# Linear attention followed by a feed-forward layer: GpSimd's tangent products moved into their own chunk, a new order of chunks 3 to 6, and batch 1's attention bursts one group later

## The chip, the cores and the metric

The kernel runs on one core of a Trainium2 chip. The metric is the time of one execution in microseconds, as the device measures it; the kernel before takes 278.01 us (median of three runs, 277.81 to 278.37). Its profiled execution took 277.38 us, of which 275.6 lie between the first and the last instruction. Positions such as "39.01" are microseconds from the first instruction.

## The reference

Eight batches, eight heads, 576 positions, head size 64. The attention is linear: ReLU on q and k, each multiplied by the cosine and by the sine of its position, then two matrix products in place of a softmax. The result is the input of a feed-forward layer with a Swish that has a factor per column.

```
theta = pi/2 * pos / S
phi(x) = concat(relu(x)*cos(theta), relu(x)*sin(theta))
kv  = phi(k)^T v ;  z = sum over positions of phi(k)
x   = (phi(q) kv) / (phi(q) z + 1e-6)          # 4608 tokens x 512
h   = x @ w_in                                  # 512 -> 2048
g   = h * sigmoid(beta * h)
out = g @ w_out                                 # 2048 -> 512
```

## The kernel before

The 4608 tokens go through the layer in 9 chunks of 512. Beside chunk c the attention of a later batch is done: its pieces are put between the groups of the layer, so that TensorE always has something to do. Names used below:

- A *group* (or slot) of the layer's first half is one tile of 128 hidden columns: four matmuls of 512 columns, then Silu on ScalarE. In chunk 0, slots 0 to 15 are these, and slots 16 to 31 are the output matmuls. From slot 24 on, slot s uses row block s - 16 of `w_out`, four matmuls of 512 columns.
- The *kv burst* (`kv_mm`) is 72 small matmuls that form phi(k)^T v of a batch; `kv_take` copies the result out of PSUM.
- The *transposes of q* (`q_turn_pe`) put q into the layout that the next step needs; the *takes* copy them out, ScalarE as they are (`qts`) and VectorE multiplied by the tangent (`qs`). In later batches the DMA transposes (`q_turn_dma`), and the tangent product is an instruction of its own (`q_tan`, two for a batch, on GpSimd).
- The *num burst* (`num_mm`, `num_all`) multiplies q by kv. The division (`x_rden`, `x_mul`, or `x_part`) follows on VectorE, and a transpose gives `xt`, the input of the layer.
- `cast_out(j)` turns block j of `w_out` from f32 to bf16, scaled by 1/beta, on VectorE, or with "a" on ScalarE.

From chunk 1 on, the products of the layer use a scheme with seven products of half size in place of eight (`o_fast`, `h_fast`), for which sums of blocks are formed on VectorE: `g_sum` (of g), `x_sum` (of x), `wh_sums` (of w_in).

The instructions of one engine keep the order in which the kernel lists them. This is batch 1's attention in chunk 0 (cuts marked):

```python
def rest():                      # called in slot 4
    ...
    load_w("out", 0); load_w("out", 1)
    load_raw(1, "v"); load_raw(1, "k"); load_raw(1, "q")
    load_w("out", 2, 2)          # blocks 8 to 11, in two loads
    load_w("out", 3, 2)
    ...
    for j in range(8):
        cast_out(j)
    v_scale(1, 0); k_relu(1)
    q_relu(1, 0); q_relu(1, 1)   # VectorE

def second():
    takes.append(q_turn_pe(1, 0, 4, hold=True))
    takes.append(q_turn_pe(1, 1, 6, hold=True))
    cast_out(8)
    takes[0]("act", 0)
    takes[0]("dve", 1)
    cast_out(9, "a")
    takes[0]("dve", 0)
    takes[0]("act", 1)
    cast_out(10)
    for e, i in (("act", 0), ("dve", 1), ("act", 1), ("dve", 0)):
        takes[1](e, i)
    for j in (11, 12, 14, 15):
        cast_out(j, "a")

for slot in range(32):
    ...
    else:                                        # slots 24 to 31
        for tt in range(4):
            o_mm(0, tt, (slot - 16,))            # reads wout block slot - 16
    ...
    if slot in early:
        early[slot]()                            # after the slot's matmuls
```

Chunk 2 begins with plain groups and ends with the two output halves x and y. Its end reads (cuts marked):

```python
y["5"](); y["c5"]()
if c == FAST - 1:
    x_sums(c + 1)
    wh_sums(12)
...
y["2"](); y["a2"]()
y["7"](); y["a7"]()              # VectorE adds out of PSUM
v_half(b + 1, 0, 5, 7)
y["3"](); y["a3"]()
v_half(b + 1, 0, 7, 9)
v_half(b + 1, 1, 3, 9, "act")
y["4"](); y["c4"]()              # the product 4 adds to the bank that a7 has read
```

Chunks 3 to 6 are given by one string of operations, `ORDER`. In it `p0` to `p7` are plain groups and `sp0` to `sp7` their Silus; `X1` to `X7` (and Y, Z, V) are the seven products of a quick pair of groups, with their copies and adds (`c1X`, `c5X`, `cuX`, `a2X`, `a3X`, `a7X`) and Silus (`SaX`, `SbX`); `K`, `kt` are the kv burst and its copy; `s01` to `s34` are the sums of g, `t1` to `t4` those of x for the next chunk; `N0` is the num burst, `x0` to `x2` the divisions; `ox1` and so on are products of the output; `k`, `q`, `v`, `w` prepare later batches; `g0`, `g1` are GpSimd's tangent products. These are held back until a named instruction is done:

```python
def q_tan(b, jp, behind=None):
    got = tan_mul(nc.gpsimd, qs_of(b)[:, jp], qts[b % 2][:, jp], 0, NQ)
    if behind is not None:
        tc.add_manual_dep(got.ins, behind.ins.name, ..., reason="GpSimd behind the sums")
```

Of the kernel before, what the change touches and what calls it, by code (L numbers as in the profile page):

```python
# [17 lines left out]
NQ = 9  # L18
# [4 lines left out]
def kernel(  # L23
# [16 lines left out]
    B, H, S, D = q.shape  # L40
# [76 lines left out]
    def cast_out(j, eng="d"):  # L117
        i, jj = divmod(j, 4)
        st = stages["out", i]
        if eng == "a":  # L120
            nc.scalar.activation(wout[:, j, :], st[:, jj, :], AF.Copy, scale=rbeta[:, j : j + 1])
        else:
            nc.vector.tensor_scalar(wout[:, j, :], st[:, jj, :],
                                    scalar1=rbeta[:, j : j + 1], scalar2=None, op0=ALU.mult)
# [141 lines left out]
    def kv_mm(b, jp, bank, jjs=(0, 1)):  # L266
        t = kv_out(jp, bank)
        for n in range(NQ):
            for jj in jjs:
                for g in range(2):  # L270
                    hs = slice(g * HP, (g + 1) * HP)
                    nc.tensor.matmul(  # L272
                        t[jj * HP : (jj + 1) * HP, g], lhsT=rk[hs, n, 2 * jp + jj, :],
                        rhs=vb[hs, n, 2 * jp + jj].rearrange("q s e -> q (s e)"),
                        start=(n == 0), stop=(n == NQ - 1))
# [382 lines left out]
    got = x_rden(2, 0, 0, 7, (0,))  # L658
# [55 lines left out]
    def num_seven(jp, bank):  # L714
        for n in range(7):
            num_mm(1, n, jp, bank, n)
# [3 lines left out]
    def second():  # L720

        takes.append(q_turn_pe(1, 0, 4, hold=True))
        takes.append(q_turn_pe(1, 1, 6, hold=True))
        cast_out(8)
        takes[0]("act", 0)
        takes[0]("dve", 1)
        cast_out(9, "a")
# [7 lines that stand above are left out]
# [1 line left out]
    early = {  # L736
        4: lambda: (num_mm(0, 8, 0, 2, 0), num_mm(0, 8, 1, 2, 1), rest()),
        15: lambda: v_scale(1, 1, eng="act"),
        22: lambda: (kv_mm(1, 0, 6), kv_mm(1, 1, 6), kv_take((0, 1), 6, "act")),
        23: second,  # L740
        25: lambda: (num_seven(0, 4), x_mul(x_rden(4, 0, 0, 7, (0,)), 0, 7), cast_out(13)),
        26: lambda: (num_seven(1, 6), x_mul(x_rden(6, 0, 0, 7, (1,)), 0, 7)),
        28: lambda: x_turn_pe(1, 0, 7, 4, ("act",), (0,)),
        29: lambda: x_turn_pe(1, 0, 7, 5, ("dve",), (1,)),
    }

    def num_rest():
# [23 lines left out]
        if b + 1 < B:  # L771
            load_raw(b + 1, "k")

    def kv_all(b, bank=6):
        kv_mm(b, 0, bank)
        kv_mm(b, 1, bank)
        kv_take((0, 1), bank)

    def x_part(b, t, bank):
        x_div(t, bank)  # L780
# [30 lines left out]
    for slot in range(16):  # L811
        h_group(1, slot)
        if slot == 0:
            num_rest()
            att_q(2)
            v_half(2, 0)
        if 3 <= slot < NQ:
            v_half(2, 1, slot, slot + 1, "act")
        if slot == 4:
            k_all(2)  # L820
            v_half(2, 1, 0, 3)
        elif slot == 6:
            w_sums()
        elif slot == 11:
            kv_all(2)
            for jp in range(2):
                tan_mul(nc.vector, qs_of(2)[:, jp], qts[0][:, jp], 0, NQ)
    q_relu(3, 0, "act")
# [28 lines left out]
    got = wh_sums(0)  # L857
# [9 lines left out]
    def k_piece(b, j):  # L867
# [4 lines left out]
            load_raw(b + 1, "k")  # L872

    ORDER = (
        "p0 Y1 X1 c1X p1 X5 c5X sp0 X6 X2 K c1Y X3 cuX kt Y6 X7 p2 a2X a3X Y5 sp1 a7X cuY c5Y Y7 Z1 SaX "
        "X4 c1Z p3 Y3 Y2 SbX sp2 a7Y Z2 s01 Y4 Z5 sp3 Z6 s03 a3Y a2Z p4 SbY V1 a2Y c5Z cuZ Z7 s02 a7Z p5 "
        "SaY c1V V6 Z3 s11 sp4 s12 cuV a3Z V2 Z4 s14 sp5 V5 SbZ c5V V7 p6 a2V V3 SaZ a7V a3V s21 sp6 SaV "
        "p7 s04 s13 V4 s22 SbV s23 sp7 s24 s31 s33 N0 k1 s32 ox1 c1o ox5 k3 c5o k2 ox6 s34 g0 g1 x0 k0 "
        "ox3 oy1 cuo c1y x2 o3x ox2 ox7 v8 oy5 x1 c5y o2x oy6 w8 q0 q1 cuy v2 v6 oy3 o7x v3 w1 oy7 w4 w3 "
        "w7 o7y ox4 v5 t3 w5 oy2 v4 c4x o3y v7 t1 w0 oy4 w6 t2 v1 c4y v0 o2y w2 t4")  # L880
    ORDER_LAST = (
        "E1 c1E E2 F1 X1 a2E c1X c1F X5 X2 E5 X6 c5X E6 cuX c5E cuE X3 a2X Y1 E3 X7 a3X c1Y a3E SaX a7X "
        "E7 SaE F6 Y5 F5 a7E X4 Y2 c5F Y6 SbX F2 F3 a2Y c5Y a2F cuF E4 Z1 Y3 cuY SbE c1Z a3F Y7 F7 a3Y "
# [40 lines left out]
    def chunk(c, b, x, y, parts):  # L924
        steady = {"X": (0, 2, 0, 1), "Y": (4, 3, 4, 5), "Z": (8, 0, 2, 1), "V": (12, 4, 3, 5)}
        end = {"X": (0, 6, 0, 1), "E": (2, 5, 3, 4), "Y": (4, 2, 0, 1), "F": (6, 7, 3, 4), "Z": (8, 6, 0, 1),
               "V": (12, 5, 3, 4)}
        pairs = {n: h_fast(c, at[0], at[1:]) for n, at in (steady if b < B else end).items()}

        def plain_bank(n):  # L930
            return (2 if n == 7 else 6 + n % 2) if b < B else (2, 7)[n % 2]

        plain = [2, 3, 6, 7, 10, 11, 14, 15]
        outs = {"x": x, "y": y}

        def q_next():
            if b + 3 < B:
                load_raw(b + 3, "q")

        def raw_next(name):  # L940
            if b + 2 < B:
                load_raw(b + 2, name)

        xs_all = {"x0", "x1", "x2"}
        take = prep(b, [
            ({"k0", "k1", "k2", "k3"} | xs_all, lambda: raw_next("k")),
            ({"q0", "q1"} | xs_all, q_next),
            ({f"{o}{n}" for o in "vw" for n in range(NQ)}, lambda: raw_next("v"))])
        last_sum = None
        for op in (ORDER if b < B else ORDER_END if c + 1 < NTC else ORDER_LAST).split():  # L950
            n = int(op[-1]) if op[-1].isdigit() else None
            if op == "K":
                kv_mm(b, 0, 4)
                kv_mm(b, 1, 4)
            elif op == "kt":
                kv_take((0, 1), 4)
            elif op[0] == "N":
                for t, bank in enumerate(parts):
                    num_all(b, t, bank)
            elif op[0] == "x":  # L960
                x_part(b, n, parts[n])
                take(op)
            elif op[0] in "kvwq":
                take(op)
            elif op[0] == "t":
                if c + 1 < NTC:
                    x_sum(c + 1, n)
            elif op[0] == "g":
                if b + 1 < B:
                    q_tan(b + 1, n, None if n else last_sum)  # L970
            elif op[0] == "p":
                h_plain(c, plain[n], plain_bank(n), 2 if n < SPLITS.get(c, (0, 0))[0] else 1)
            elif op[:2] == "sp":
                h_silu(c, plain[n], plain_bank(n))
            elif op[0] == "o" and n is not None:
                outs[op[1]][op[2]]()
            elif op[0] == "o":
                outs[op[2]]["a" + op[1]]()
            elif op[0] == "c" and op[2] in "xyo":
                outs["x" if op[2] == "o" else op[2]][op[:2]]()  # L980
            elif op[0] == "s":
                last_sum = g_sum(c, 2 * int(op[1]), 2 * int(op[1]) + 2, n)
            else:
                pair = op[0] if op[0] in pairs else op[-1]
                pairs[pair][op.replace(pair, "")]()
        if b + 2 < B:
            q_turn_dma(b + 2)

    def h_first(c):
        b = c + 1  # L990
        for slot in range(16):
            h_group(c, slot, 2 if slot < SPLITS.get(c, (0, 0))[0] else 1)
            if c == 2:
                if slot == 0:
                    k_all(b)
                    v_half(b, 1, 0, 4)
                if 1 <= slot < 6:
                    v_half(b, 1, slot + 3, slot + 4, "act")
                if slot == 3:
                    att_q(b + 1)  # L1000
                    wh_sums(4)
                if slot == 9:
                    wh_sums(8)
            if slot == (8 if c == 2 else 1):
                kv_all(b)
            if slot in (3, 7, 11):
                g_sums(c, slot // 2 - 1, slot // 2 + 1)
            elif slot in (13, 15):
                sums = g_sums(c, slot // 2, slot // 2 + 1)
        return sums  # L1010

    FAST = 3
    for c in range(2, NTC):
# [4 lines left out]
        if c >= FAST:  # L1018
            chunk(c, b, x, y, parts)
            continue  # L1020
        sums = h_first(c)
        for t, bank in enumerate(parts):
            num_all(b, t, bank)
        q_tan(b + 1, 0, sums)
        q_tan(b + 1, 1)
        for i, n in enumerate("156273"):
            x[n]()
            if n in "156":
# [15 lines left out]
        y["c5"]()  # L1044
        if c == FAST - 1:
            x_sums(c + 1)
            wh_sums(12)
        v_half(b + 1, 1, 2, 3, "act")
        y["6"]()
        y["cu"]()  # L1050
# [5 lines left out]
        y["3"]()  # L1056
        y["a3"]()
        v_half(b + 1, 0, 7, 9)
        v_half(b + 1, 1, 3, 9, "act")
        y["4"]()  # L1060
        y["c4"]()
# [31 lines left out]
```

## Time and profile before

| what | value |
|---|---|
| time, median of three | 278.01 us |
| span of the profiled execution | 275.6 us |
| busy: TensorE, VectorE, ScalarE, GpSimd | 268.9, 221.0, 184.6, 67.8 us |
| mean granted clock of TensorE | 1.000 |
| one tangent product of a batch half | 2.38 us on GpSimd, 1.35 on VectorE |

How to read the profile lines that follow. A timeline line has the start, the time from the start to the end of the last of the merged instructions, the engine, the line of the kernel, the operation, what it writes and reads, the shapes, and the number of instructions. In brackets stand the idle time of the engine ahead of it and the instruction that ended that idle time. Matmuls are pipelined, so one matmul's stated duration is longer than the distance to the next; the distance is what counts. `PE` is TensorE, `DVE` VectorE, `ACT` ScalarE, `POOL` GpSimd, and `SP` issues DMAs.

### The profile page before, as it was taken

The numbers are of one execution on the slowest core, as the hardware profiler recorded it, in microseconds if no ns is written. First come the engines' busy times: TensorE is split into PE (matmuls) and PEld (weight loads), VectorE is DVE, ScalarE is ACT, GpSimd is POOL, SyncE is SP. The second block draws the span as 40 slices with busy tenths as digits, with TensorE's granted clock in tenths as the row PEclk, the third lists the DMA queues.
The fourth block names the chain that finished last, engine by engine and source line by source line (L and its number), as shares of the span: only waits on it lengthen the run. The fifth ranks groups of instructions, "written<-read, shape, count | busy, mean of one in ns | idle before, by whom it ended". The sixth has DMA issues, their size and how long they took to land.

```text
span 275.6 us, 9047 instructions
## 1 busy us (share of the span) xinstructions
PE 268.9 (98%) x3749; PEld 199.8 (73%) x3749; DVE 221.0 (80%) x578; ACT 184.6 (67%) x381; POOL 67.8 (25%) x87
## 2 busy tenths in 40 slices
PE   8899999999999999999999999999999999999993
PEld 8554455446875599869866998688768886888683
DVE  5989968599999898599959995899589589558851
ACT  5778757797248657697669756976694289429821
POOL 1444000600087073106420552044300140000000
PEclk9999999999999999999999999999999999999999
DMA  7999999999969999961899199915400640033005
GB/s 248 369 394 382 393 389 312 375 193 377 244 153 309 245 309 295 394 130 38 179 359 267 39 220 301 121 21 107 114 2 12 117 115 2 0 70 86 2 24 130
DMA packets 50745, 54.00 MB, mean 196 GB/s; under 512 B 31232, under 2 KB 31760, under 8 KB 50704
## 3 DMA queue, kind: packets, MB, share of 16 engines
q1 hardware_dynamic: 47744, 45.88, 59.5%
q0 software_dynamic: 2688, 7.34, 8.9%
q8 instruction: 29, 0.48, 0.7%
q10 hardware_dynamic: 272, 0.21, 0.3%
q14 instruction: 12, 0.10, 0.2%
HBM read 36.71 MB, written 9.44 MB: 167 GB/s over the span
## 4 chain that ended last, share of the span: by engine, by line
PE 83%; DMA 12%; DVE 2%; ACT 1%; SPq 1%; issue 0%; ACTq 0%; DVEq 0%
PE ps L547 35%; PE ps L468 16%; PE ps L422 13%; PE ps L380 10%; DMA raw_q<-in_q_dram 7%; DMA w_stage<-in_moe_w_in_dram 5%; PE ps L293 4%; PE ps L517 3%; PE ps L272 2%; DVE win L115 1%; ACT vb L217 1%; SPq L79 1%; PE ps L234 0%; PE ps L352 0%; DVE qb L194 0%
## 5 line engine op out<-in xcount | busy, mean ns | idle before, releaser
L413 ACT ACTIVATE g_t<-ps,beta 128x512 bf16<-128x512 f32 x96 | 61.0, 698 | 3.1 <-DVE ps L498 2.8
L547 PEld LDWEIGHTS <-S 128*128 128x128 bf16 x589 | 51.3, 98 | 5.0
L510 POOL DMA_DIRECT2D out_dram<-o_sb x56 | 33.5, 604 | 66.3 <-ACT o_sb L523 24.6
L380 PE MATMUL ps<-xt,win 128*128 128x512 bf16 (+1 forms) x196 | 42.8, 375 | 0.1
L547 PEld LDWEIGHTS <-g_t 128*128 128x128 bf16 x440 | 38.2, 98 | 4.3 <-issue 0.3
L422 PE MATMUL ps<-xt,win 128*128 128x512 bf16 (+1 forms) x184 | 40.8, 351 | 0.0
L388 ACT ACTIVATE g_t<-ps,beta 128x512 bf16<-128x512 f32 x48 | 32.2, 690 | 8.0 <-PE ps L380 7.8
L380 PEld LDWEIGHTS <-win 128*128 128x128 bf16 x196 | 18.8, 98 | 21.0 <-issue 0.4
L547 PE MATMUL ps<-wout,g_t 128*128 128x256 bf16 (+1 forms) x284 | 31.7, 262 | 0.0
L547 PE MATMUL ps<-wout,S 128*128 128x256 bf16 (+1 forms) x305 | 31.5, 255 | 0.0
L547 PE MATMUL ps<-T,S 128*128 128x256 bf16 (+1 forms) x284 | 30.8, 262 | 0.0
L399 DVE TENSOR_TENSOR S<-g_t 128x512 bf16<-128x512 bf16 (+1 forms) x66 | 25.1, 409 | 3.6 <-ACT g_t L413 2.7
L217 ACT ACTIVATE vb<-raw_v,sin 128x256 bf16<-128x256 f32 (+1 forms) x61 | 27.4, 501 | 0.9 <-DMA raw_v<-in_v_dram 0.9
L222 POOL TENSOR_TENSOR qs<-qt,tanr 128x1152 bf16<-128x1152 bf16 x6 | 14.2, 2382 | 50.8 <-DVE den L304 29.8
L468 PEld LDWEIGHTS <-w_stage 128*128 128x128 bf16 x224 | 21.6, 98 | 6.7
L468 PE MATMUL ps<-w_stage 128*128 128x256 bf16 x168 | 26.2, 272 | 0.0
L422 PEld LDWEIGHTS <-win 128*128 128x128 bf16 x184 | 17.9, 98 | 10.1
L315 DVE TENSOR_TENSOR xs<-ps,rden 128x768 bf16<-128x768 f32 (+4 forms) x26 | 22.8, 883 | 0.8
L219 DVE TENSOR_SCALAR vb<-raw_v,cos 128x256 bf16<-128x256 f32 x63 | 20.5, 380 | 0.1
L468 PEld LDWEIGHTS <-win 128*128 128x128 bf16 x168 | 16.4, 98 | 4.8 <-issue 0.3
L468 PE MATMUL ps<-xt,win 128*128 128x256 bf16 x112 | 19.1, 273 | 0.0
L594 ACT COPY p<-ps 128x256 f32<-128x256 f32 x16 | 6.0, 373 | 17.0 <-PE ps L547 16.9
(105 smaller groups left out, 417.6 us busy)
## 6 DMA issues: line engine op xcount, KB each, us to landing
raw_v<-in_v_dram SPq DMA_DIRECT2D x7, 1152.0 KB, 9.9
raw_k<-in_k_dram SPq DMA_DIRECT2D x7, 1152.0 KB, 7.5
raw_q<-in_q_dram SPq DMA_DIRECT2D x7, 1152.0 KB, 7.7
out_dram<-o_sb POOLq DMA_DIRECT2D x56, 128.0 KB, 4.4
w_stage<-in_moe_w_in_dram SPq DMA_DIRECT2D x3, 1024.0 KB, 13.0
w_stage<-in_moe_w_out_dram SPq DMA_DIRECT2D x2, 1024.0 KB, 8.1
w_stage<-in_moe_w_out_dram SPq DMA_DIRECT2D x4, 512.0 KB, 11.9
out_dram<-o_sb SPq DMA_DIRECT2D x12, 128.0 KB, 2.4
```

The costliest lines, as they stand in the source:

```text
L217: nc.scalar.activation(o, a, AF.Copy, scale=t[:, n : n + 1])
L219: nc.vector.tensor_scalar(o, a, scalar1=t[:, n : n + 1], scalar2=None, op0=ALU.mult)
L222: return eng.tensor_tensor(dst.rearrange("q n (g p) -> q n g p", g=2), src.rearrange("q n (g p) -> q n g p", g=2), tanr[:, n0:n1].unsqueez ...
L315: nc.vector.tensor_tensor(o.rearrange("q j n s d -> q j (n s) d"), nv[:, :, a:z, :, 0:D].rearrange("q j n s d -> q j (n s) d"), rden[:, :, ...
L380: nc.tensor.matmul(ps[:, h_bank(c, jt), i * 64 : (i + w) * 64], lhsT=win[jt // 4][:, mi, (jt % 4) * P : (jt % 4 + 1) * P], rhs=xt[:, i : i ...
L388: nc.scalar.activation(gs[c, jt // 4][:, jt % 4], ps[:, h_bank(c, jt)], AF.Silu, scale=beta[:, jt : jt + 1])
L399: return nc.vector.tensor_tensor(o, l, r, op=op)
L413: nc.scalar.activation(gs[c, jt // 4][:, jt % 4], ps[:, bank], AF.Silu, scale=beta[:, jt : jt + 1])
L422: nc.tensor.matmul(ps[:, bank, o * 64 : z * 64], lhsT=win[jt // 4][:, mi, (jt % 4) * P : (jt % 4 + 1) * P], rhs=xt[:, o:z, jp, g * HP : (g ...
L468: nc.tensor.matmul(dst, lhsT=left[:, g], rhs=right[:, :, g * HP : (g + 1) * HP], start=start and g == 0, stop=stop and g == 1, skip_group_ ...
L510: (eng or own).dma_start(out=out_v[bb, n][:, m0:m1], in_=o_sb[hf * HP : (hf + 1) * HP, m0:m1])
L547: nc.tensor.matmul(dst[:, m : m + w], lhsT=left(i), rhs=right[:, i, m : m + w], start=start and i == 0, stop=stop and i == order[-1], skip ...
```

## The change

GpSimd's two tangent products of a batch were made in the output stage of the chunk before, behind the last sum of g. Now they are made in the batch's own chunk, near its beginning, behind the copy `c5X`, at a time when VectorE works out of PSUM. The string for chunks 3 to 6 is a new one with the same operations. In chunk 0, the kv burst of batch 1, its q transposes, num bursts and x transposes each move one slot later, so that a late arrival of q does not hold them up; `cast_out(8)`, which slot 24 needs, moves ahead of slot 24. In chunk 1 the kv burst of batch 2 moves one slot earlier and its copy from VectorE to ScalarE, and two scalings of v from ScalarE to VectorE. At the end of chunk 2 `wh_sums(12)` moves behind the adds.

The diff, cut to its core:

```diff
@@ second()
         takes.append(q_turn_pe(1, 0, 4, hold=True))
         takes.append(q_turn_pe(1, 1, 6, hold=True))
-        cast_out(8)
         takes[0]("act", 0)
@@ early
-        22: lambda: (kv_mm(1, 0, 6), kv_mm(1, 1, 6), kv_take((0, 1), 6, "act")),
-        23: second,
-        25: lambda: (num_seven(0, 4), x_mul(x_rden(4, 0, 0, 7, (0,)), 0, 7), cast_out(13)),
-        26: lambda: (num_seven(1, 6), x_mul(x_rden(6, 0, 0, 7, (1,)), 0, 7)),
-        28: lambda: x_turn_pe(1, 0, 7, 4, ("act",), (0,)),
-        29: lambda: x_turn_pe(1, 0, 7, 5, ("dve",), (1,)),
+        23: lambda: (kv_mm(1, 0, 6), kv_mm(1, 1, 6), kv_take((0, 1), 6, "act"), cast_out(8)),
+        24: second,
+        26: lambda: (num_seven(0, 4), x_mul(x_rden(4, 0, 0, 7, (0,)), 0, 7), cast_out(13)),
+        27: lambda: (num_seven(1, 6), x_mul(x_rden(6, 0, 0, 7, (1,)), 0, 7)),
+        29: lambda: x_turn_pe(1, 0, 7, 4, ("act",), (0,)),
+        30: lambda: x_turn_pe(1, 0, 7, 5, ("dve",), (1,)),
@@ chunk 1
-        if 3 <= slot < NQ:
-            v_half(2, 1, slot, slot + 1, "act")
+        if 2 <= slot < 6:
+            v_half(2, 1, slot + 3, slot + 4, "act")
         if slot == 4:
             k_all(2)
-            v_half(2, 1, 0, 3)
+            v_half(2, 1, 0, 5)
-        elif slot == 11:
-            kv_all(2)
+        elif slot == 10:
+            kv_all(2, eng="act")
@@ ORDER (first and last words of the old and of the new string)
-        "p0 Y1 X1 c1X p1 X5 c5X sp0 X6 X2 K c1Y X3 cuX kt Y6 X7 p2 a2X a3X Y5 sp1 a7X cuY c5Y Y7 Z1 SaX "
...
-        "p7 s04 s13 V4 s22 SbV s23 sp7 s24 s31 s33 N0 k1 s32 ox1 c1o ox5 k3 c5o k2 ox6 s34 g0 g1 x0 k0 "
...
-        "w7 o7y ox4 v5 t3 w5 oy2 v4 c4x o3y v7 t1 w0 oy4 w6 t2 v1 c4y v0 o2y w2 t4")
+        "Y1 p1 X1 c1Y p0 X2 c1X X6 Y6 X5 cuY a2X K cuX c5X sp0 X7 kt X3 a3X p2 sp1 Y5 SaX Y7 sp2 a7X Y2 X4 Z1 c5Y "
+        "SbX a2Y Y3 a3Y p3 a7Y Z5 c1Z c5Z V1 Y4 SaY Z6 s01 Z2 Z3 sp3 s03 p4 cuZ SbY Z7 V2 a3Z V5 c1V g0 g1 a2Z "
...
+        "oy2 o2y t1 t2 t3 c4x oy4 t4 c4y")
@@ chunks 3 to 6
             elif op[0] == "g":
-                if b + 1 < B:
-                    q_tan(b + 1, n, None if n else last_sum)
+                if b < B:
+                    q_tan(b, n, None if n else first)      # first: the instruction of c5X
@@ chunk 2
-        q_tan(b + 1, 0, sums)
-        q_tan(b + 1, 1)
@@ end of chunk 2
         if c == FAST - 1:
             x_sums(c + 1)
-            wh_sums(12)
...
         v_half(b + 1, 0, 7, 9)
+        wh_sums(12)
         v_half(b + 1, 1, 3, 9, "act")
```

## The prediction

> **What bounds the kernel now.** I read in this order: the page's busy times, the busy time by stretch, the timeline of TensorE between 38 and 52 us, the timelines of VectorE and ScalarE beside it, and the landing of one weight load.
>
> ```profile
> PE 268.9 (98%) x3749; PEld 199.8 (73%) x3749; DVE 221.0 (80%) x578; ACT 184.6 (67%) x381; POOL 67.8 (25%) x87
> ...
> PE 83%; DMA 12%; DVE 2%; ACT 1%; SPq 1%; issue 0%; ACTq 0%; DVEq 0%
> ```
>
> The matmul row is busy 98% of 275.6 us, and the chain that ended last runs through TensorE for 83%; nearly all the rest of the chain is the DMA of the first 40 us. A busy matmul row is no proof that TensorE streams at its best, so I compare one chunk with the sum of its matmuls.
>
> ```profile
> 109.20:137.20 28.00, 28.00 (x433) 23.26 (x431) 22.62 (x63) 20.56 (x44) 9.41 (x10) 1.00 0.68 189
> 137.20:165.30 28.10, 28.10 (x474) 22.58 (x472) 23.34 (x65) 20.96 (x45) 9.48 (x11) 1.00 0.84 225
> ```
>
> Columns: stretch, length, busy time of TensorE, weight loads, VectorE, ScalarE, GpSimd, granted clock, DMA share, GB/s. A chunk of batch 4 or later needs 8 plain groups of 4 matmuls of 512 columns (44 of these take 9.60 us in the chain of waits, so 0.218 each: 6.98), 4 x 7 quick products of 2 matmuls of 256 columns (0.109 each: 6.10), the kv burst (1.15 + 0.13 of drain), the num burst (1.38 + 0.12), and 2 x 7 x 8 output matmuls at 0.109 (12.21): 28.07 us, and 28.0 to 28.1 are measured. **Chunks 3 to 6 stand at their floor**: a new order can't gain there, it can only lose. VectorE and ScalarE are busy 75 to 85% of a chunk, so a bad order could make TensorE wait.
>
> What TensorE loses outside is small. Batch 1's attention in chunk 0 has two waits:
>
> ```profile
> 37.86 1.22 PE L272 MATMUL ps<-vb,rk 64*64 64x130 bf16 x72
> 39.01 1.04 PE L517 MATMUL ps<-wout,g_t 128*128 128x512 bf16 x4
> ...
> 40.10 1.34 PE L234 MATMUL ps<-ident,qb 128*128 128x128 bf16 x18
> 41.28 1.89 PE L517 MATMUL ps<-wout,g_t 128*128 128x512 bf16 x8
> ```
>
> The four matmuls of group 23 begin at 39.01 and stream 0.87 us, so the transposes of q could begin at 39.88; they begin at 40.10. They need 18 x 0.057 = 1.02 us, and take 1.18. The two waits are 0.22 and 0.16, **0.38 us**. Their cause is VectorE:
>
> ```profile
> 39.28 1.43 DVE L194 TENSOR_SCALAR qb<-raw_q 128x1152 bf16<-128x1152 f32 x2 [1.64 <-DMA raw_q<-in_q_dram]
> 40.64 0.48 DVE L123 TENSOR_SCALAR wout<-w_stage,rbeta 128x512 bf16<-128x512 f32 x1
> 41.04 1.41 DVE L222 TENSOR_TENSOR qs<-ps,tanr 128x512 bf16<-128x512 bf16 x2
> 42.37 0.48 DVE L123 TENSOR_SCALAR wout<-w_stage,rbeta 128x512 bf16<-128x512 f32 x1
> ```
>
> raw_q lands at 39.26 (issued at 24.45, 14.81 us in the chain), and then come two ReLUs of q. The line at 40.64 is the cast of wout block 8, the weights of output group 24. It stands behind the ReLUs, and its own data come late too:
>
> ```profile
> 26.57 7.75 SPq L101 DMA_DIRECT2D w_stage<-in_moe_w_out_dram  x4
> ...
> DMA to landing us min/median/max: 14.0/14.0/14.0
> ```
>
> The load issued at 26.57 holds blocks 8 and 9 and lands 14.0 us later, at 40.6. So block 8 is ready at 41.12, **whatever is moved around it**. Group 24 begins at 41.28, so today this is just in time.
>
> The other loss is at the end of chunk 2: the last product of the second half begins at 108.16 although the matmuls before it were issued by 107.79 (54 ns each). It waits 0.31 us for the add that ends at 108.10:
>
> ```profile
> 107.15 0.29 DVE L448 TENSOR_TENSOR w_stage<-win,w_stage 128x256 bf16<-128x256 bf16 x1
> 107.36 0.42 DVE L597 TENSOR_TENSOR o_sb<-ps,p 128x256 f32<-128x256 f32 x1
> 107.69 0.41 DVE L599 TENSOR_TENSOR o_sb<-ps,p 128x256 f32<-128x256 f32 x1
> ```
>
> [...] under the GpSimd products of 76.56 to 81.28 the adds out of PSUM keep their 0.41 us, but four scalings of v begun at 79.46 take 2.77 instead of some 1.1. [...] the cast of block 8 comes when both ReLUs are through. [...]
>
> **The change, part by part.** No instruction is added or removed in number on TensorE; only places move.
>
> *Attention of batch 1, one group later.* The kv burst now follows group 23, and the transposes follow group 24 instead of 23. Group 24 needs block 8. TensorE therefore reaches group 24 after the kv burst at 39.01 + 0.87 = 39.88 and waits for the cast: 41.12 + 0.06 (the delay between the second ReLU's end at 40.71 and TensorE's next step at 40.77) = 41.18. **First wait 1.30 us**, in place of the 0.38.
>
> Next, group 25 needs block 9, which ScalarE casts after its first copy of the transposes:
>
> ```profile
> 40.59 0.69 ACT L239 COPY qt<-ps 128x640 bf16<-128x640 bf16 x1 [0.50 <-PE ps L234]
> 41.18 0.72 ACT L121 ACTIVATE wout<-w_stage,rbeta 128x512 bf16<-128x512 f32 x1
> 41.80 1.17 ACT L239 COPY qt<-ps 128x512 bf16<-128x512 bf16 x2
> 43.48 0.59 ACT L239 COPY qt<-ps 128x512 bf16<-128x512 bf16 x1 [0.51 <-DVE qs L222]
> 43.96 2.56 ACT L121 ACTIVATE wout<-w_stage,rbeta 128x512 bf16<-128x512 f32 x4
> ```
>
> From the transposes' start (40.10) to block 9 (41.90) are 1.80 us. Today group 24 fills that time; after the change group 25 follows the 1.02 us of transposes at once. They begin at 41.18 + 0.87 = 42.05, block 9 is there at 43.85, TensorE at 43.07: **second wait some 0.84 us** with the 0.06. Block 10 follows VectorE's two tangent takes: they start some 0.73 after the transposes (42.78), the cast is at +1.33 (41.04 to 42.37) and ends near 44.6, before group 26 (44.8). Group 27 needs block 11, ScalarE's first cast after four copies; the last copy waits for VectorE's third take. From VectorE's first take to that cast's end were 43.96 + 0.72 - 41.04 = 3.64 us, so it ends near 46.4; TensorE, after groups 25 and 26 and 0.58 us of num products, is there at 46.2: **third wait some 0.25 us**. Later casts and the two turns of x keep their distances. Sum: 1.30 + 0.84 + 0.25 - 0.38 = **+2.0 us**. Everything after is bound by TensorE, so nothing gives it back.
>
> *Sums of weights later at the end of chunk 2.* The four sums (0.93 us, 106.43 to 107.36) leave the place ahead of the two adds. The second add can then start when its product is through, near 107.15, and ends near 107.6, before TensorE needs it at 107.84: **-0.31 us**.
>
> *GpSimd's products in their own chunk.* Two products, 4.73 us, leave the output stage. There they lie beside PSUM work; they cost a scaling of v 0.2 us (0.55 instead of 0.34, at 131.00) that nobody waits for. They now start behind the copy c5X: six quick products (1.31) and two plain groups (1.74) come first, then about 0.6 for the copy and 0.24 to start GpSimd (126.43 to 126.67): from 3.9 to 8.6 us in the chunk. VectorE then works on PSUM; the first sum of two SBUF tiles is due near 8.6, and the num products near 14.3. **0.0 us.**
>
> *New order in chunks 3 to 6; chunk 1's kv copy on ScalarE.* The orders hold the same operations. Laid out with the trace's durations, each matmul of the new order finds its inputs and its bank some tenths before its turn, as in the old. **0.0, with 0.1 us either way for each chunk.**
>
> Sum: 278.01 + 2.0 - 0.3 = 279.7 us.
>
> **The rivals.** (a) *The move works as meant*: the 0.38 us go and no wait comes in their place, 277.3 us. It needs block 8 by 39.9; a landing at 40.6 and the place behind the ReLUs speak against it. (b) *Only the first wait comes*, because ScalarE or VectorE catch up: 278.01 + 0.92 - 0.3 = 278.6. (c) *The new order is worse*: one late tile of 0.3 us in each of four chunks makes 281. The full VectorE speaks for it, the similar distances against. (d) *GpSimd runs into the sums*: if the products end a microsecond late, the first sum blocks, and some of that reaches TensorE: up to 1 us in all. (e) *VectorE has more room and the chunks become faster*: they are at the floor, so no.
>
> **Range and chances.** The size of the wait for block 8 rests on a landing in one trace, perhaps 0.3 us off; the second and third waits on distances carried over; the chunks on 0.4 in all. I put 279.7, with 278.5 to 280.7. Two per cent are 5.6 us, out of reach for any of these: faster 0.01, within 0.97, slower 0.02.
>
> **What would show it.** In the new profile: TensorE idle before group 24 for over a microsecond, released by VectorE's cast (L123); again before group 25, by ScalarE (L121); chunk 1 beginning near 52.4 instead of 50.34. No wait at the end of chunk 2. Chunks of 28.0 to 28.1 us, with GpSimd's products at their beginning. I'd be wrong if block 8 landed a microsecond earlier, or if a chunk grew above 28.3.

## The result, and the profile after

The changed kernel takes **279.54 us** (median of four runs, 279.02 to 279.88), the kernel before 278.12 us (median of four, 277.81 to 278.37). The ratio is **1.005, with a 95% interval of 1.0029 to 1.0071**: half a per cent slower, and more than the measurement is uncertain. The prediction was 279.7 us.

The profiled execution of the changed kernel has a span of 278.0 us, 2.4 more than before's 275.6. The page, its line of busy times and the line of the chain that ended last by engine:

```profile
PE 266.8 (96%) x3745; PEld 198.5 (71%) x3749; DVE 222.4 (80%) x579; ACT 184.3 (66%) x380; POOL 66.8 (24%) x87
...
PE 84%; DMA 9%; DVE 4%; SPq 1%; ACT 1%; issue 1%; ACTq 0%; DVEq 0%
```

The span grew and TensorE's busy time did not, so the growth is waiting. DVE's share of the chain went from 2% to 4%. The waits of TensorE, by the line that waited and the line that released it (us in all, times, longest), show where:

```profile
PE ps L517 <- DVE wout L123: 1.9, 1, 1.9
...
PE ps L517 <- ACT wout L121: 0.8, 2, 0.7
```

L517 are the output groups of chunk 0, L123 and L121 the casts of `w_out`, on VectorE and on ScalarE. Neither line is in this view of the kernel before. The timeline of TensorE gives their places:

```profile
38.40 1.22 PE L272 MATMUL ps<-vb,rk 64*64 64x130 bf16 x72
41.48 1.02 PE L517 MATMUL ps<-wout,g_t 128*128 128x512 bf16 x3 [1.87 <-DVE wout L123]
42.34 1.17 PE L234 MATMUL ps<-ident,qb 128*128 128x128 bf16 x18
44.19 1.89 PE L517 MATMUL ps<-wout,g_t 128*128 128x512 bf16 x8 [0.68 <-ACT wout L121]
...
46.82 1.02 PE L517 MATMUL ps<-wout,g_t 128*128 128x512 bf16 x3 [0.17 <-ACT wout L121]
...
52.60 1.03 PE L380 MATMUL ps<-xt,win 128*128 128x512 bf16 x4
```

These are the three waits of the prediction, in their order and with their releasers: group 24 for block 8, group 25 for block 9, group 27 for block 11. The bracket counts from the listed end of the last matmul; a matmul of 512 columns is listed with 0.38 us, where the next one begins 0.218 later, so the stream itself stood still a little longer. The 72 matmuls of the kv burst take 1.15 (37.86 to 39.01 in the kernel before), so TensorE was free at 38.40 + 1.15 = 39.55 and stood 1.93 us until 41.48. The transposes take 1.02, so it was free again at 43.36 and stood 0.84 (rounded) until 44.19. The third, reckoned in the same way, is 0.24. Chunk 1 begins at 52.60; before it began at 50.34.

Beside it, the timelines of VectorE and of ScalarE:

```profile
39.59 1.43 DVE L194 TENSOR_SCALAR qb<-raw_q 128x1152 bf16<-128x1152 f32 x2 [1.64 <-DMA raw_q<-in_q_dram]
40.94 0.49 DVE L123 TENSOR_SCALAR wout<-w_stage,rbeta 128x512 bf16<-128x512 f32 x1
```

```profile
42.82 0.69 ACT L239 COPY qt<-ps 128x640 bf16<-128x640 bf16 x1 [2.19 <-PE ps L234]
43.41 0.72 ACT L121 ACTIVATE wout<-w_stage,rbeta 128x512 bf16<-128x512 f32 x1
```

The cast of block 8 is now listed ahead of group 24, and still runs right behind the two ReLUs of q, at the time when its data came (40.92). Both hold it to the same moment: the second ReLU ends at 41.02, and VectorE began it 0.08 before the end of the first, so that it could begin the cast near 40.94 at the soonest. The cast of block 9 stands behind ScalarE's first copy of the transposes.

Busy time by stretch, one chunk each from about the end of chunk 2 on (columns as in the prediction):

```profile
111.40:139.43 28.03, 27.94 (x430) 23.17 (x429) 23.28 (x64) 20.50 (x45) 7.69 (x9) 1.00 0.67 186
139.43:167.63 28.20, 28.20 (x475) 22.61 (x473) 23.60 (x64) 20.85 (x45) 9.04 (x11) 1.00 0.82 213
167.63:195.66 28.03, 28.03 (x427) 22.68 (x425) 23.86 (x69) 20.86 (x45) 8.96 (x11) 1.00 0.56 156
```

The distances from one chunk's first output product to the next chunk's, for chunks 3 to 6, are 28.03, 28.20 and 28.03 us, where the old order had 27.98, 28.15 and 27.98. So nearly the whole loss lies ahead of chunk 1: +2.26 at its first matmul, +2.2 at the outputs of chunk 2, +2.4 at the end.

### The profile page after: what moved, and what is told of

It reads as the page before. It is cut to its first block, busy times and chain, and to the rows that moved or that the text cites. A ratio compares the mean times of both kernels' runs of the same rounds, so it can differ in the third digit from the quotient of the medians.

```text
span 278.0 us, 9048 instructions
## 1 busy us (share of the span) xinstructions
PE 266.8 (96%) x3745; PEld 198.5 (71%) x3749; DVE 222.4 (80%) x579; ACT 184.3 (66%) x380; POOL 66.8 (24%) x87
## 4 chain that ended last, share of the span: by engine, by line
PE 84%; DMA 9%; DVE 4%; SPq 1%; ACT 1%; issue 1%; ACTq 0%; DVEq 0%
PE ps L547 35%; PE ps L468 16%; PE ps L422 12%; PE ps L380 12%; DMA raw_q<-in_q_dram 6%; PE ps L293 4%; DMA raw_v<-in_v_dram 3%; PE ps L272 2%; PE ps L517 2%; SPq L79 1%; DVE xs L315 1%; DVE qs L222 1%; DVE qb L194 1%; PE ps L352 0%; DVE win L115 0%
## 5 line engine op out<-in xcount | busy, mean ns | idle before, releaser
L510 POOL DMA_DIRECT2D out_dram<-o_sb x56 | 32.6, 588 | 119.9 <-DVE o_sb L597 74.0
L547 PE MATMUL ps<-wout,S 128*128 128x256 bf16 (+1 forms) x305 | 32.2, 255 | 0.0
L547 PE MATMUL ps<-T,S 128*128 128x256 bf16 (+1 forms) x284 | 31.4, 262 | 0.0
L399 DVE TENSOR_TENSOR S<-g_t 128x512 bf16<-128x512 bf16 (+1 forms) x66 | 25.5, 411 | 2.8 <-ACT g_t L413 1.9
L217 ACT ACTIVATE vb<-raw_v,sin 128x256 bf16<-128x256 f32 (+1 forms) x59 | 25.9, 501 | 2.1 <-DMA raw_v<-in_v_dram 2.1
L468 PE MATMUL ps<-w_stage 128*128 128x256 bf16 x168 | 26.9, 273 | 0.0
L468 PE MATMUL ps<-xt,win 128*128 128x256 bf16 x112 | 20.4, 272 | 0.0
L219 DVE TENSOR_SCALAR vb<-raw_v,cos 128x256 bf16<-128x256 f32 x63 | 19.5, 375 | 0.8 <-DMA raw_v<-in_v_dram 0.8
L496 DVE TENSOR_TENSOR ps<-ps,p 128x256 f32<-128x256 f32 x28 | 11.9, 429 | 7.4 <-PE ps L468 5.9
```

The costliest lines, as they stand in the source:

```text
L217: nc.scalar.activation(o, a, AF.Copy, scale=t[:, n : n + 1])
L219: nc.vector.tensor_scalar(o, a, scalar1=t[:, n : n + 1], scalar2=None, op0=ALU.mult)
L399: return nc.vector.tensor_tensor(o, l, r, op=op)
L468: nc.tensor.matmul(dst, lhsT=left[:, g], rhs=right[:, :, g * HP : (g + 1) * HP], start=start and g == 0, stop=stop and g == 1, skip_group_ ...
L510: (eng or own).dma_start(out=out_v[bb, n][:, m0:m1], in_=o_sb[hf * HP : (hf + 1) * HP, m0:m1])
L547: nc.tensor.matmul(dst[:, m : m + w], lhsT=left(i), rhs=right[:, i, m : m + w], start=start and i == 0, stop=stop and i == order[-1], skip ...
```

## The experiments

Theory: the moved bursts cost some 2 us, through the casts of `w_out`, and nothing else in the change matters. Rivals: the new order or GpSimd costs it; the loss is another one that only looks like the three waits; the loss is partly given back by something later that was late anyway. The quoted expectations were written before the runs. Differences below a few tenths of a us are beyond these timings: the timed runs of the kernel before alone lie between 276.8 and 281.1 us.

**Undo the bursts** (the changed kernel with the old slots and the old `second()`).

```diff
-        23: lambda: (kv_mm(1, 0, 6), ..., cast_out(8)),
-        24: second,          # and 26, 27, 29, 30
+        22: lambda: (kv_mm(1, 0, 6), ...),
+        23: second,          # and 25, 26, 28, 29; cast_out(8) in second() again
```

> The changed kernel with only the attention bursts of batch 1 back in their old slots (22, 23, 25, 26, 28, 29, and the cast of block 8 behind the transposes). Theory 1, the waits for wout blocks 8, 9 and 11 are the whole loss: TensorE waits 0.4 us at the transposes instead of 3.0 us in three places, the time falls by 2 us or so against the changed kernel and lies at 277.7 to 278.1. Theory 2, the new order of chunks 3 to 6 costs something of its own: 278.5 or more.

Measured: 278.28 us, ratio to before 1.0008 (0.9993 to 1.0022). Chunk 1 begins at 50.30 again. The loss is gone, so **it is the bursts**. The change to chunk 1 was not run alone; it is in this kernel, together with the order and the sums, and the three leave the time where it was. They don't lower it either, and the trace shows a wait that was not expected. TensorE at the end of chunk 2, and ScalarE beside it:

```profile
107.59 0.60 PE L547 MATMUL ps<-wout,S 128*128 128x256 bf16 x7 [1.51 <-ACT u L595]
```

```profile
105.43 0.52 ACT L217 ACTIVATE vb<-raw_v,sin 128x256 bf16<-128x256 f32 x1 [2.51 <-DMA raw_v<-in_v_dram]
```

ScalarE waits 2.51 us for the load of v of batch 4, and the copy that TensorE needs stands behind it in ScalarE's queue. In this execution TensorE runs into a load that is not there yet. In the kernel before it comes as early and doesn't: there v landed at 103.3, here at 105.4.

**The bursts alone** (the kernel before with the new slots and the new `second()`, nothing else).

```diff
-        22: lambda: (kv_mm(1, 0, 6), ...),
-        23: second,
+        23: lambda: (kv_mm(1, 0, 6), ..., cast_out(8)),
+        24: second,          # and 26, 27, 29, 30
```

> The kernel before with only the bursts moved one slot later. Theory 1: the three waits (about 1.9, 0.84 and 0.25 us) appear in full, chunk 1 begins near 52.5 instead of 50.3, the time is 279.7 to 280.2. Theory 2: less than 1 us is added, below 279.1, and the rest of the loss comes from the chunks.

Measured: 280.26 us, ratio 1.0087 (1.0064 to 1.011). Chunk 1 begins at 52.33. TensorE's waits in this kernel:

```profile
PE ps L517 <- DVE wout L123: 1.2, 1, 1.2
...
PE ps L517 <- ACT wout L121: 0.9, 2, 0.7
```

The same pair of lines as in the changed kernel, with no other part of the change in it. Its median lies 0.7 us above the changed kernel's. The runs of the other two parts alone don't explain that, and its profiled span, 277.8, is no longer than the changed kernel's. With six runs, and intervals of the ratio that overlap, it may be scatter; it stays open.

**The order alone** (the kernel before with the new string and with GpSimd's products in their own chunk).

```diff
-                if b + 1 < B:
-                    q_tan(b + 1, n, None if n else last_sum)
+                if b < B:
+                    q_tan(b, n, None if n else first)
@@ chunk 2
-        q_tan(b + 1, 0, sums)
-        q_tan(b + 1, 1)
```

> The kernel before with only the new order of chunks 3 to 6 and GpSimd's products in their own chunk. Theory 1: the chunks are at their floor in both, 278.1 with at most 0.3 us more (a wait of 0.1 us in the third part of each num burst). Theory 2: over 0.5 us more or less.

Measured: 278.27 us, ratio 1.0006 (0.9989 to 1.0022); chunks 28.04, 28.20 and 28.04. Neither gain nor loss that could be told from zero.

**The sums alone** (the kernel before with `wh_sums(12)` behind the adds).

```diff
             x_sums(c + 1)
-            wh_sums(12)
...
         v_half(b + 1, 0, 7, 9)
+        wh_sums(12)
```

> The kernel before with only the four weight sums at the end of chunk 2 moved behind the adds. Theory 1: the wait of 0.31 us ahead of the last product of chunk 2 goes, nothing comes in its place: 0.3 us less, 277.8. Rival: chunk 3 gives it back through later work on VectorE, as the profile of the changed kernel (28.57 us from the first output product of chunk 2 to that of chunk 3, against 28.52 before) may be read: no difference.

Measured: 278.33 us, ratio 0.9993 (0.997 to 1.0015). In its trace the last product starts without a wait, and the distance from the outputs of chunk 2 to those of chunk 3 is 28.25, where before has 28.52: −0.27 us. The time does not show it; an interval of 0.45% is 1.2 us wide. Two of the fourteen runs, the profiled one (281.32 us) among them, were slow; without them the median is 278.12, and of this trace only that one stretch, at a granted clock of 1.00, is compared.

**Block 9 first** (the changed kernel, with ScalarE's cast of block 9 ahead of its copies).

```diff
+        cast_out(9, "a")
         takes[0]("act", 0)
         takes[0]("dve", 1)
-        cast_out(9, "a")
```

> The changed kernel with the cast of wout block 9 moved ahead of ScalarE's first copy of the transposes, so that output group 25 needn't wait for it (0.84 us in the changed kernel). Theory A, what sets the end is the chain from the transposes through VectorE's takes and ScalarE's fourth copy to the cast of block 11: group 25 starts 0.8 us sooner, but groups 26 and 27 wait for blocks 10 and 11 instead, chunk 1 begins where it did (52.6, within 0.15), and the time is the same as the changed kernel's. Theory B, the waits simply add: 0.8 us less, 278.7.

Measured: 279.72 us, ratio 1.0061 (1.004 to 1.0082); chunk 1 begins at 52.43. TensorE's timeline:

```profile
43.18 1.03 PE L517 MATMUL ps<-wout,g_t 128*128 128x512 bf16 x4
44.82 1.02 PE L517 MATMUL ps<-wout,g_t 128*128 128x512 bf16 x4 [0.61 <-DVE wout L123]
```

Group 25 at 43.18 no longer waits, and group 26 waits for block 10 in its place, then group 27 for block 11. The whole stage hangs on a chain that begins with the transposes and runs through the takes to block 11 (the theory called A), not on any one cast: **taking away one wait moved it on**.

**Blocks 9, 10 and 11 first** (the changed kernel, all three casts ahead of the takes).

```diff
+        cast_out(9, "a")
+        cast_out(10)
+        cast_out(11, "a")
         takes[0]("act", 0)
         takes[0]("dve", 1)
-        cast_out(9, "a")
...
-        cast_out(10)
...
-        for j in (11, 12, 14, 15):
+        for j in (12, 14, 15):
```

> The changed kernel with the casts of blocks 9, 10 and 11 all ahead of the copies of the transposes. The blocks land at 40.9 (9) and 42.3 (10, 11), and both engines stand idle then for the transposes. Both theories: the second and third wait (0.84 and 0.25 us) go, group 27 no longer waits, the first wait for block 8 stays (1.9 us in the profile): 1.0 us less than the changed kernel, 278.5. Rival: the copies come later and the num bursts wait for them, less than 0.4 us gained.

Measured: 279.17 us, ratio 1.003 (1.0011 to 1.0049). Both later waits are gone and chunk 1 begins at 51.22, so the chain is confirmed: 52.60 − 51.22 = 1.4 us in the profiled runs, of which 0.84 + 0.24 = 1.1 are the two waits. The medians show only 0.4 to 0.55 of it. But the medians of these small groups are uncertain by as much: in ratios, this kernel is 0.0031 ± 0.0028 below the run with block 9 first, measured beside it, or 0.9 us, where chunk 1 begins 52.43 − 51.22 = 1.2 earlier. So the timings don't say that less comes through to the end.

**The weights loaded ahead of q**, with the casts first.

```diff
+        load_w("out", 2, 2)
         load_raw(1, "q")
-        load_w("out", 2, 2)
...
+        cast_out(8)
         q_relu(1, 0)
```

> casts_first, and the load of wout blocks 8 and 9 issued ahead of batch 1's q, the cast of block 8 ahead of the ReLUs. Theory: the landing sets the first wait. Blocks 8 and 9 land near 37.9 and q near 40.9; group 24 starts right behind the kv burst; the transposes wait for q's first ReLU instead, 1.1 to 1.3 us, and 0.16 between the halves. In all 1.4 us of waits against 3.0: 1.5 us less than the changed kernel, 278.0. Rival: moving the load only trades one wait for another of the same length, 278.5 as with casts_first.

Measured: 280.49 us, ratio 1.0085 (1.0062 to 1.0108), chunk 1 at 53.62. A miss, by its construction: this call issues two loads, blocks 8 and 9 and blocks 10 and 11. Both now stood ahead of q, which landed at 41.99. On TensorE's timeline group 24 needs no wait any more, and the transposes have it:

```profile
42.83 2.10 PE L234 MATMUL ps<-ident,qb 128*128 128x128 bf16 x18 [2.07 <-DVE qb L194]
```

The late q is only a third of the loss, though. Chunk 1 begins 2.4 later than with the three casts first (51.22), but the transposes 0.8 (42.83 against 42.02). The rest comes behind the wait, where TensorE's granted clock is low (the last column but two):

```profile
42.90:45.00 2.10, 2.10 (x19) 1.97 (x20) 1.86 (x4) 0.89 (x2) 0.00 (x0) 0.50 0.53 90
45.00:48.00 3.00, 2.90 (x64) 1.40 (x64) 1.87 (x4) 2.85 (x6) 0.00 (x0) 0.81 0.93 335
```

By estimate that costs 2.1 x 0.50 + 3.0 x 0.19 = 1.6 us, and the distances agree: the 18 transposes and the 8 matmuls of groups 25 and 26 take 4.43 us here (42.83 to 47.26) and 2.83 with the casts first (42.02 to 44.85). The run does show that group 24's wait goes when block 8 is loaded ahead of q, there by 37.63, and cast ahead of the ReLUs. It moves both at once; that its load alone made the wait is not shown, and in the changed kernel the ReLUs held the cast to the same moment.

**GpSimd gated by the sums** (the changed kernel, with the products held back until the first sum of g, not the copy c5X).

```diff
-                got = pairs[pair][op.replace(pair, "")]()
-                if op == "c5X":
-                    first = got
+                if op == "s01":      # the first sum of g
+                    first = got
```

> The changed kernel with GpSimd's products held until the first sum of g (s01) instead of the copy c5X, so that they run from about 9.2 to 13.9 us of the chunk, beside sums with both inputs in SBUF. Theory 1, place matters: either the sums beside them stretch from 0.42 us to up to 2.4 each, or the products stretch past 14.3 us, where the num burst needs them; the num burst or the first output product waits, and each of chunks 3 to 6 grows by 1 us or more (283 or more). Theory 2, there is no conflict to speak of: the sums keep 0.42 us, the chunks 28.0 to 28.2, 279.5.

Measured: 292.51 us, ratio 1.0506 (1.0419 to 1.0593), 2.7 to 4.1 us for each of four chunks. The timelines of VectorE and of TensorE, while GpSimd's two products run from 152.77 to 157.67:

```profile
153.67 1.76 DVE L399 TENSOR_TENSOR S<-g_t 128x512 bf16<-128x512 bf16 x1
...
155.69 2.26 DVE L399 TENSOR_TENSOR S<-S,g_t 128x512 bf16<-128x512 bf16 x1
157.87 0.41 DVE L494 COPY p<-ps 128x256 f32<-128x256 f32 x1
```

```profile
158.34 0.38 PE L468 MATMUL ps<-xt,w_stage 128*128 128x256 bf16 x2 [2.13 <-DVE p L494]
```

A sum of two SBUF tiles that takes 0.42 us alone takes 1.76 and 2.26 beside GpSimd; the copy out of PSUM behind it is late by as much, and TensorE waits for that copy. Between them an add out of PSUM (155.35) keeps its 0.42. The wait is only part of the price. By stretch, the last column but two is TensorE's granted clock:

```profile
155.00:158.40 3.40, 1.02 (x7) 0.53 (x6) 3.40 (x5) 1.77 (x3) 2.67 (x2) 1.00 1.28 126
158.40:162.00 3.60, 3.60 (x46) 1.67 (x49) 3.56 (x11) 1.62 (x3) 0.00 (x0) 0.66 0.09 18
```

After 3.4 us in which TensorE was busy for 1.02, its clock is 0.66 over the next 3.6 us, which by estimate costs 3.6 x 0.34 = 1.2 us more; eight matmuls of 512 columns take 2.42 us there (158.55 to 160.97), 8 x 0.218 = 1.74 elsewhere. But such a wait stands in all four chunks (8.5 us in all), and over two of them, the first and the last, the mean clock is 1.00, over the two others 0.95. The two at 1.00 are the ones that grew least, by 3.4 and 2.7 us. So the place of the products **matters**, and the place that the change chose is free.

**v earlier, bursts undone** (the first experiment, with the attention step that transposes q moved from slot 3 to slot 6 of chunk 2).

```diff
                 if slot == 3:
-                    att_q(b + 1)
                     wh_sums(4)
+                if slot == 6:
+                    att_q(b + 1)
```

What stood ahead of the load of v is in the DMA queue's timeline of the first experiment:

```profile
87.16 7.54 SPq L252 DMA_TRANSPOSE qt<-qb  x1
94.79 0.53 SPq L79 DMA_DIRECT2D raw_q<-in_q_dram  x1
95.41 0.46 SPq L79 DMA_DIRECT2D raw_v<-in_v_dram  x1
```

Issuing the transposes of q occupies SP's queue for 7.54 us, and v, issued behind them, lands 10.0 later.

> burst_back (the changed kernel with the bursts in their old slots) and, in chunk 2, the ReLU and transpose of batch 4's q three groups later (slot 6 instead of 3), so that batch 4's v is asked for ahead of the long transpose issue (near 87 us instead of 95.4) and lands near 97 instead of 105.4. Theory M, the late landing of v at the end of chunk 2 masks a part of what is won or lost before it: ScalarE's wait for v (2.5 us) and TensorE's wait behind it (1.68 us in burst_back's profile) go, and the time falls by 1 to 1.6 us to 276.7 to 277.3. Rival N, that wait was a chance of one profile: no change, 278.2.

Measured: 277.55 us, ratio 0.9987 (0.9971 to 1.0003), and the same view:

```profile
86.47 0.37 SPq L79 DMA_DIRECT2D raw_v<-in_v_dram  x1
89.47 6.60 SPq L252 DMA_TRANSPOSE qt<-qb  x1
```

v is issued 8.9 us earlier, nothing waits for it at the end of chunk 2, and the distance to the outputs of chunk 3 falls from 29.94 to 28.36. By its median it is the fastest of all kernels here, 2.0 us under the changed kernel; against the kernel before, the interval just includes 1. The two traces are not of like executions, though. The times of both kernels fall into two groups: without the edit, 10 of 22 runs are under 277.7 and 12 over 278.2, with it 12 under 277.7 and 10 over 278.0. The first trace is from the upper group (278.80), the second from the lower (277.14). With v early the upper group is still there, so a late v alone does not make it, and the means differ by less than the medians, 278.11 and 277.85: 0.26 ± 0.22 us (standard error).

**v earlier, bursts moved** (the changed kernel with the same edit), and **the changed kernel again** in the same group.

> The changed kernel with the same step in chunk 2. Theory M: its TensorE comes to the end of chunk 2 some 2 us later and waited little or not at all for v, so it gains under 0.5 us (279.0 to 279.6), and its distance to v_early_back is the full cost of the moved bursts, 2.0 to 2.4 us, more than the 1.3 between the changed kernel and burst_back. Rival N: the distance stays at 1.3.

> The changed kernel, unchanged, on the same chip as the three others, for their distances: 279.5, 1.4 us over the kernel before.

Measured: 279.57 us, ratio 1.005 (1.0034 to 1.0066), and 279.59 us, ratio 1.0046 (1.0024 to 1.0068). With v early in both, the moved bursts cost 279.57 − 277.55 = **2.0 us**, the sum that the prediction had. With v late in both, they cost 279.59 − 278.28 = 1.3. In ratios these are 0.0063 ± 0.0023 and 0.0038 ± 0.0026 (the intervals' halves, added in squares). 2.0 us are 0.0072: inside the first interval and outside the second. The two overlap, so the timings don't prove a difference. By means there is hardly one: 279.69 − 277.85 = 1.8 with v early, 279.80 − 278.11 = 1.7 with v late, and 280.19 − 278.19 = 2.0 for the bursts alone, each with a standard error of 0.2 to 0.25. A median that lies between two groups jumps by the gap when two runs change sides. The theory called M, that the late v hides part of the bursts' cost, is therefore not shown. Of eleven profiled executions with v late, only the one above has TensorE waiting over a microsecond behind it.

In the second run of the changed kernel, the kv burst began at 39.16, 0.76 later than in the first, and the first wait in the list of waits was 0.9 instead of 1.9; chunk 1 began at 52.35, only 0.25 away. The length of the first wait says when TensorE came; its end, which the cast of block 8 sets, is what counts.

**Both causes removed in chunk 0**: v early, only blocks 8 and 9 loaded ahead of q, casts early, the transposes one slot later again.

```diff
+        load_w("out", 2, 2, 0, 2)          # blocks 8 and 9
         load_raw(1, "q")
-        load_w("out", 2, 2)
+        load_w("out", 2, 2, 2, 4)          # blocks 10 and 11
...
-        23: lambda: (kv_mm(1, 0, 6), ..., cast_out(8)),
-        24: second,
+        23: lambda: (kv_mm(1, 0, 6), ..., cast_out(9, "a")),
+        25: second,
```

> v_early_after with the first waits taken away too: wout blocks 8 and 9 (one load of 0.5 MB, not the two of load_first) are loaded ahead of batch 1's q, blocks 8 to 11 are cast as soon as they land, and the transposes of q follow group 25. Blocks 8 and 9 should land near 37.7 and q near 40.7; groups 24 and 25 run while q lands; the transposes wait 0.1 to 0.5 us, the first num burst some 0.3. Chunk 1 begins near 50.2 instead of 52.6, and the time is that of v_early_back or 0.2 less, 276.6 to 277.2. Rival: q lands as late as in load_first (42.0), waits of over 1 us, 278 or more.

Measured: 278.76 us, ratio 1.0004 (0.9988 to 1.0021), chunk 1 at 50.96. A miss of some 2 us in the time and 0.8 in chunk 1. The load of blocks 8 and 9 was there by 37.50, when VectorE cast block 8, but the cast of block 9 was listed behind the copy of kv on ScalarE, which starts at 40.23, and came at 40.72:

```profile
41.49 1.02 PE L517 MATMUL ps<-wout,g_t 128*128 128x512 bf16 x4 [0.72 <-ACT wout L121]
```

Group 25 came before it, and the num burst then waited 0.38 for a take. So chunk 1 began 1.4 us earlier than with the bursts moved (52.33), and the order in ScalarE's queue kept the rest. The profiled execution took 277.79, close to the shortest of the fourteen runs (277.70); why the median is a microsecond longer is not explained.

## Why the prediction was right, point by point

- **Chunks at their floor.** Right. Predicted 28.0 to 28.1, measured 28.03, 28.20, 28.03. All kernels with the new order and GpSimd in place give these values, +0.05 each on the old: within the tenth allowed, and not visible in time.
- **The first wait, 1.30.** Right in place, cause and releaser; the trace has 1.93. TensorE was through with the kv burst at 39.55 instead of 39.88 (0.33), and the load came at 40.92 instead of 40.61 (0.31, the size that the prediction's range allowed for such a landing); q came 0.30 later too. Only the second of these moves chunk 1. That block 8 is ready at 41.12 "whatever is moved around it" was too strong: with its load ahead of q and its cast ahead of the ReLUs it was ready at 38.12.
- **The second, 0.84, and the third, 0.25.** Right within 0.02 in the changed kernel's trace, and again in the bursts alone. Carrying distances over from the old trace worked, since the chain from the transposes through the takes to the casts is the same. That it is one chain is shown by the run with block 9 first.
- **Chunk 1 near 52.4.** Measured 52.60 and 52.35 in two executions of the changed kernel, and 52.33 with the bursts alone.
- **−0.31 at the end of chunk 2.** The mechanism is right: in the changed kernel the adds come at 108.87 and 109.43, and the last product starts at 110.06 without a wait.

```profile
108.87 0.42 DVE L597 TENSOR_TENSOR o_sb<-ps,p 128x256 f32<-128x256 f32 x1
109.43 0.42 DVE L599 TENSOR_TENSOR o_sb<-ps,p 128x256 f32<-128x256 f32 x1
...
110.06 1.05 PE L547 MATMUL ps<-T,g_t 128*128 128x256 bf16 x15
```

  The gain is not in the total: from chunk 2's outputs to chunk 3's, the changed kernel takes 28.57, before 28.52. A pause of 0.27 between two small matmuls of the num burst of chunk 3 (at 126.53) and 0.1 in its third part took it back. Such a pause stands in a num burst of the kernel before too (0.22, at 68.68), and the profile shows no instruction that ends either; their cause stays open. With v early and the bursts moved, the last product waits 0.29 again.
- **GpSimd, 0.0.** Right. GpSimd's timeline and the sums' line in the view of L399 (shortest, median and longest in ns):

```profile
143.13 4.73 POOL L222 TENSOR_TENSOR qs<-qt,tanr 128x1152 bf16<-128x1152 bf16 x2 [0.68 <-PE ps L468]
```

```profile
L399 DVE TENSOR_TENSOR S<-S,g_t x33: 285/419/428, 70.2 to 264.1; 128x512 bf16<-128x512 bf16 x31, 128x256 bf16<-128x256 bf16 x2
```

  The products begin about where predicted, keep their 4.73 us, and not one sum is stretched. Rival (d), a run into the sums, was a real danger: it put "up to 1 us in all" on an overlap of a microsecond, and with all 4.9 us of the products beside the sums it costs 13. What one microsecond of overlap costs was not run.
- **"Everything after is bound by TensorE, so nothing gives it back."** Not refuted, and not shown to the tenth. In one execution with the bursts undone 1.5 us went to a wait for a v that had not landed; but the cost of the bursts by means is 2.0 in the kernel before, 1.7 in the changed kernel and 1.8 with v early, which the runs don't tell apart from the 2.0 that the prediction had.

So the mechanism was right: three waits, in their places, with their releasers, make the loss. That 279.7 met 279.54 within 0.2 us is in part luck. In the profiled pair the change costs 2.4 us, in the timed medians 1.4, and the prediction's sum of 1.7 lies between; the gain of 0.31 did not come through; and the bursts alone cost 2.1 by their median. Rival (b), only the first wait, at 278.6, was ruled out by the second and third; rivals (c) and (e) by the chunks' distances.

## What to carry to other kernels

Before delaying a consumer to make room for late data, look at what is put ahead of it: here group 24 was pulled in front of q's transposes, and its own weights land later than q. When a wait is removed, follow what is listed behind it on each engine to the next operation in the chain: in the last run block 9, there by 37.50, was cast at 40.72, behind the copy of kv. Before a difference of medians is read as a cost, look at the single times: where they fall into two groups, the median can jump by the gap between them, and one trace shows one of the groups. And look at what VectorE does while GpSimd works on SBUF: here an add out of PSUM kept its 0.42 us beside GpSimd's products, sums of two SBUF tiles took 1.76 and 2.26 in place of 0.42, and moving the products a few microseconds, beside those sums, cost 5%.

## What the runs showed of the hardware that was not expected

- Issuing the DMA transposes of q occupied SP's queue in chunk 2 for 5.30 us in the kernel before, 5.70 in the changed kernel, 7.54 with the bursts undone and 6.60 with v early as well (9.4 to 10.5 us for the next batch's), and the loads listed behind it were issued only then. Moving them behind the load of v brought that load forward by 8.9 us.
- The load of v of batch 4, behind the same entries of SP's queue, was issued at 94.0 and landed at 103.3 in the kernel before, and at 95.4 and 105.4 in the bursts undone, although chunk 1 began at the same time (50.34 and 50.30). The transposes ahead of it began at 87.27 and 87.16 and took 5.30 and 7.54 us; why they differ was not tested. A single trace is no firm ground for the landing of a load in mid-kernel.
- Behind a wait of about 2 us on TensorE its granted clock was low in some places and 1.00 in others. With GpSimd beside the sums, four waits of 2.1 us came with a mean clock of 0.95 over two of the chunks (0.66 for 3.6 us behind the wait in one of them) and of 1.00 over the two others. Behind 2.07 us in chunk 0 of the run with the weights loaded ahead of q it was 0.50, then 0.81, and the next 26 matmuls took 1.6 us longer than with the casts first. Behind 1.87 us in chunk 0 of the changed kernel, and 1.51 with the bursts undone, it was 1.00. So the length of the wait alone does not decide, and what does was not tested.
